# Gated linear attention and two feed-forward layers on one core: right-hand SBUF tiles moved by 32 bytes, and a new set of planned times

## The chip, the cores and the metric

The kernel runs on one core of a Trainium2 chip. The metric is device time in microseconds; lower is better. The kernel before takes 1009.64 us, the median of three runs (1009.35 to 1015.21).

## The reference: what is computed

Three layers, one after the other, on 4 sequences of 768 tokens (3072 tokens in all):

1. Attention with a decaying state, 8 heads of 48: `state = alpha_t * state + k_t v_t^T`, `y_t = q_t state`.
2. A feed-forward layer, 384 to 2048 to 384. Its inner function is a rational one: with `h = x @ w_in`, `g = (a0 + a1 h + a2 h^2 + a3 h^3) / (1 + |b0||h| + |b1| h^2 + 1e-6)`, and the result is `g @ w_out`.
3. A gated feed-forward layer, 384 to 1536 to 384: `silu(x @ w_gate) * (x @ w_val) @ w_out`.

Inputs are random; the weights and `a`, `b` of layer 2 and the weights of layer 3 arrive as 64-bit floats.

## The kernel before, in words

**Work.** Attention is cut into 24 chunks of 128 tokens. For each chunk TensorE turns alpha, k and q around (`tr`, L655), VectorE scans alpha forwards and backwards (L671, L679) and scales k and q (`kt` L687, `qt` L697). TensorE then forms the scores (`scores`, L706), turns `kt` back (`back`, L731) and, in `values`, forms the update of the state (`upd`, L750), scores times v (L755) and state times q (L761). The result goes to DRAM (`xd`).

Layer 2 (`moe1`) takes blocks of 512 tokens. The float32 values are split into a high and a low part, so that each product of float32 matrices is three TensorE products (`mm3`, L840 to L842). One inner tile `f` of a block costs 9 products of 512 columns for `h`, whose streamed (moving) operand is `xt`, some fifteen operations on ScalarE, VectorE and GpSimd, and 9 products of 512 columns for `acc`, whose moving operand is `gg`. The result goes to DRAM (`y1d`).

Layer 3 (`moe2`) takes the same blocks: 72 rounds (6 blocks times 12 inner tiles). A round is 9 products of 512 columns into `pg`, 9 into `pv`, both with `yy` as the moving operand, and 12 products of 384 columns into `po` (L1079 to L1081) with the weights `wo` as the moving operand and `pp` as the stationary one.

**A check beside it.** `bounds` reads alpha and all weights once more: 80 loads named `chk` (L971, 12 of alpha and 68 of weights) into a ring of three buffers. VectorE counts the values in a usable range. For a load of weights these are one extraction (L1013, `chk_e`) and two counts (L984). At the end it sums the counts (L1020, L1021), one small TensorE product adds the partitions (`pf`, L1023), and L1025 writes a `flag`. After the last instruction of the three layers every engine reads the flag (L1197) and branches on it (L1200) past a general program that does not run here.

**Memory.** Pools are opened on the left or the right side of SBUF. On the left lie constants, the 32 weight slots, `xt`, `gg` and the other tiles of `moe1`. On the right lies first `ap` (attention) and, when attention is done, `pb` in its place (`yr`, `yy`, `sg`, `pp` of layer 3). For the first two chunks `kt`, `aa0`, `aa1` and `kn` lie in weight slots on the left (`room`, `early`), later on the right. In the compiled kernel the right side ends at byte 229,344 of a partition, 32 past a multiple of 64; `yr`, `yy`, `sg` and `pp` all start 32 past a multiple of 64, and `xt` and `gg` on one. In `ap` the five tiles of 516 or 517 floats take 2080 bytes each, so that tiles there start partly on multiples of 64, partly 32 past one; `qt` and the later `kt`, `aa` and `kn` start 32 past one.

**Order of the work.** No engine's order is written by hand. Every operation is given to a `Plan` with an engine, a planned duration, what it reads and writes, and a planned time `v`. From these `order` works out a due time for each operation, moved by a bias for its group ("w" weights, "att", "x", "moe"). It then runs a clock of its own: at each step it takes the engine that can start earliest, and on it the operation with the earliest due time among those that are ready by the planned durations. An operation with two possible engines may take the second one only within `THETA` of the lateness of TensorE. The instructions are issued in the order of these planned starts. All engines then work down their queues on the chip, SyncE's DMA queue included, where an issue waits for its tile and holds up those behind it.

One kind of operation also has an absolute floor on that clock, `not_before`: load number k of the check is not planned before `begin + (v - begin) * k / 80`, where

```python
flag = bounds(end_a + 103.59, vs2[-1][0] - 20.0)
```

`vs2[-1][0]` is the planned time of the first round of the last block: `end_a + 5.14 + 60 * P2`, with `P2 = 6.45`. A planned check load lasts 1.1 and is taken to be usable 2.1 later.

The tables `cv` (one planned time for each chunk), `vs` (one for each inner tile of each segment of `moe1`), `MM2`, `EV`, `end_a`, `THETA` and the biases are numbers found by a fit.

Of the kernel before, what the change touches and what calls it, by code (L numbers as in the profile page):

```python
# [9 lines left out]
F32 = mybir.dt.float32  # L10
# [3 lines left out]
ALU = mybir.AluOpType  # L14
# [5 lines left out]
PE, DVE, ACT, POOL, DMA = range(5)  # L20
CAPS = {"w": 99, "early": 9, "att": 3, "h": 5, "acc": 3, "po": 4, "g": 4, "tr": 1, "cv": 1}
HOP = {PE: 0.22, DVE: 0.2, ACT: 0.2, POOL: 0.15, DMA: 2.1}
SAME = {PE: 0.0, DVE: 0.07, ACT: 0.09, POOL: 0.05, DMA: 2.1}
THETA = 48.61


class Buf:
# [7 lines left out]
class Plan:  # L35
# [51 lines left out]
    def order(self):  # L87
# [46 lines left out]
        def ready(e, c):  # L134
            r = c[3]
            if c[2]:
                r = max(r, c[0] + late - THETA)
            if e == DVE and c[4]:
# [216 lines left out]
def gla_moe_moe2_kernel(  # L355
# [15 lines left out]
    nc = tc.nc  # L371
    ctx.enter_context(tc.manual_schedule())
    B, H, S, D = q.shape
# [3 lines left out]
    C = 128  # L377
    C1 = C + 1
    NP = H // 2
    L = NP * C1  # L380
    R = 64 + D
# [13 lines left out]
    plan = Plan()  # L395
    main = ExitStack()
# [4 lines left out]
    ps = main.enter_context(tc.tile_pool(name="ps", bufs=1, space=PSUM))  # L401
    xp = tc.tile_pool(name="xp", bufs=1)
    mp = tc.tile_pool(name="mp", bufs=1)
    ap = tc.tile_pool(name="ap", bufs=1, side="right")
    pb = tc.tile_pool(name="pb", bufs=1, side="right", reuse_waits="tile")
    pb2 = tc.tile_pool(name="pb2", bufs=1, reuse_waits="tile")
# [16 lines left out]
    def new(pool, shape, dt, tag, bufs=1, name=None):  # L423
        b = plan.buf(
            lambda: pool_of(pool).tile(shape, dt, tag=tag, bufs=bufs, name=name or tag), f"{pool}.{tag}", bufs
        )
        if not b.before:
            b.before = after.get(pool, ())
        return b

    def fixed(t):
        b = plan.buf(None)
        b.t = t
        return b
# [26 lines left out]
    A = pools["ap"]  # L461
    NBV = 2
    nat = {}
    for nm in "akqv":
        for i in range(NBV if nm == "v" else 1):
            t = A.tile([128, H, 64], F32, name=f"nat{nm}{i}")
            nc.gpsimd.memset(t[:, :, D:64], 1.0 if nm == "a" else 0.0)
            nat[nm, i] = fixed(t)
    al, seed_f, seed_r = (fixed(A.tile([128, L + 1], F32, name=x)) for x in ("al", "seed_f", "seed_r"))
    for t in (al, seed_f, seed_r):  # L470
        nc.gpsimd.memset(t.t, 0.0)
    nc.gpsimd.memset(seed_f.t[:, 0:L:C1], 1.0)
# [11 lines left out]
    def quad(t):  # L484
        return t.rearrange("p (n c) -> p n c", c=128)
# [148 lines left out]
    def attention(v0, dv, m):  # L634
# [3 lines left out]
        first, last = m % NC == 0, m % NC == NC - 1  # L638
# [11 lines left out]
        def tr(vv, src, name):  # L650
            p4 = bank("tr", name)

            def f():
# [8 lines left out]

        aT = tr(v0, na, "aT")
        plan.op(v0, [(ACT, 0.48, lambda: nc.scalar.copy(per(al.t, 1), quad(aT.t)[0:R]))], (aT,), (al,))
        bb = new("ap", [128, L], F32, "bb")
        bC = new("ap", [128, NP], F32, "bC", 2)
        cc = new("ap", [128, L + 1], F32, "cc")
        kT = tr(v0 + dv, nk, "kT")
        plan.op(
            v0,  # L670
            [(DVE, 1.15, lambda: nc.vector.tensor_tensor_scan(  # L671
                bb.t[0:R], al.t[0:R, 0:L], seed_f.t[0:R, 0:L], 0.0, ALU.mult, ALU.add), True)],
            (al, seed_f), (bb,),
        )
        plan.op(v0, [(DVE, 0.1, lambda: nc.vector.reciprocal(seed_r.t[0:R, C1 : L + 1 : C1], bb.t[0:R, C:L:C1]))],
# [4 lines left out]
                cc.t[0:R, L:0:-1], al.t[0:R, L:0:-1], seed_r.t[0:R, L:0:-1], 0.0, ALU.mult, ALU.add), True)],  # L680
            (al, seed_r), (cc,),
        )
        plan.op(v0, [(ACT, 0.1, lambda: nc.scalar.copy(bC.t[0:R], bb.t[0:R, C:L:C1]))], (bb,), (bC,))
        kt = room("kt")
        plan.op(
            v0 + dv,
# [7 lines left out]
        qt = new("ap", [128, NP, 128], F32, "qt", 2)  # L694
# [6 lines left out]
        sc = [bank("att", f"sc{g}") for g in range(2)]  # L701
# [6 lines left out]
                    start=True, stop=True,  # L708
                )

        plan.op(v0 + 3 * dv, [(PE, 1.1, scores)], (kt, qt), tuple(sc))
        for g in range(2):
            plan.op(
                v0 + 4 * dv,
# [10 lines left out]
        if not last:  # L725
            kn_ps = bank("att", "kn_ps")
            kn = room("kn")

            def back():
                for p in range(NP):  # L730
                    nc.tensor.transpose(quad(kn_ps.t)[:, p, 0:R], kt.t[0:R, p, :], ident[0:R, 0:R])  # L731

            plan.op(v0 + 4 * dv, [(PE, 0.52, back)], (kt,), (kn_ps,))
            plan.op(v0 + 4 * dv, [(ACT, 0.48, lambda: nc.scalar.copy(kn.t[:, :, 0:R], quad(kn_ps.t)[:, :, 0:R]))], (kn_ps,), (kn,))
        yT = bank("att", "yT")
        upd = None if last else bank("att", "upd")
# [4 lines left out]
        def values():  # L741
# [21 lines left out]
                    )  # L763

        plan.op(
            v0 + 5 * dv, [(PE, (0.0 if first else 1.1) + (0.2 if last else 0.7) + 0.9, values)],
            (vn, *aa, qt) + (() if first else (st_s,)) + (() if last else (kn,)), (yT,) + (() if last else (upd,)),
        )
        yo = new("ap", [128, NP, 128], F32, "yo")
# [8 lines left out]
        if last:  # L778
            return
        def bCx():  # L780
            return bC.t[0:R].unsqueeze(2).to_broadcast((R, NP, D))

        if first:
            plan.op(v0 + 6 * dv, [(DVE, 0.27, lambda: nc.vector.tensor_tensor(st_c.t[0:R], u4(), bCx(), ALU.mult))],
# [59 lines left out]
    def moe1(vs, n, part, f0, f1, xt, win, wout):  # L844
# [58 lines left out]
        def second(f, gg):  # L903
# [5 lines left out]

            plan.op(vs[f - f0] + MM2, [(PE, 9 * (T / 2400 + 0.0135), mm2)], (wout[f], gg), tuple(acc))  # L910

# [5 lines left out]
        for z in pend:  # L917
            second(*z)
        vl = vs[-1] + MM2
        for j in range(NJ):  # L920
            ys = new("mp", [128, TMAX], F32, "ys", YS)
            yc = cut_(ys, T)
            if part == 0:
                how = [act(T, lambda j=j, yc=yc: nc.scalar.copy(yc(), acc[j].t[:, 0:T]), 0, False),
                       dve(T, lambda j=j, yc=yc: nc.vector.tensor_copy(yc(), acc[j].t[:, 0:T]))]
                plan.op(vl - EV, how, (acc[j],), (ys,))
            else:
# [104 lines left out]
    def moe2(vs, n, f0, f1, yy, wg, wv, wo):  # L1032
        po = [bank("po", f"po{t}") for t in range(CPB)]

        def first(f):
            v = vs[f - f0]
            pg, pv = bank("g", "pg"), bank("g", "pv")
            for pz, w in ((pg, wg[f]), (pv, wv[f])):

                def gv(pz=pz, w=w):  # L1040
                    for j in range(NJ):
                        s = slice(j * 128, (j + 1) * 128)
                        y = yy[j].t
                        mm3(pz.t, w.t[:, 0, s], w.t[:, 1, s], y[:, 0], y[:, 1], j == 0, j == NJ - 1)

                plan.op(v, [(PE, 2.05, gv)], (w, *yy), (pg, pv) if pz is pg else (pv,))

            cuts = 2 if n == NT // TB - 1 and f == F2 - 1 else 1
            r = []
            for c in range(cuts):  # L1050
                w = TB // cuts
                d = 1 / cuts
                z = slice(c * w, (c + 1) * w)
                sg = new("pb", [128, TB], F32, "sg", 2)
                pp = new("pb", [128, 2, TB], F32R, "pp", 2)
                plan.op(v, [(ACT, 0.08 + 0.42 * d, lambda sg=sg, z=z: nc.scalar.activation(sg.t[:, z], pg.t[:, z], AF.Silu))],  # L1056
                        (pg,), (sg,), last_exp)
                plan.op(v, [(DVE, 0.07 + 0.53 * d, lambda sg=sg, z=z: nc.vector.tensor_tensor(  # L1058
                    sg.t[:, z], sg.t[:, z], pv.t[:, z], ALU.mult))], (sg, pv), (sg,))
                plan.op(v, [(ACT, 0.1 + 0.43 * d, lambda sg=sg, pp=pp, z=z: nc.scalar.copy(pp.t[:, 0, z], sg.t[:, z]))],  # L1060
                        (sg,), (pp,))
                plan.op(
                    v,
                    [(DVE, 0.07 + 0.53 * d, lambda sg=sg, pp=pp, z=z: nc.vector.tensor_tensor(
                        pp.t[:, 1, z], sg.t[:, z], pp.t[:, 0, z].bitcast(F32), ALU.subtract), True)],
                    (sg, pp), (pp,),
                )
                r.append(pp)
            return r

        def second(f, r):
            k = CPB // len(r)
            for c, pp in enumerate(r):

                def mm4(c=c, pp=pp):
                    for t in range(c * k, (c + 1) * k):
                        s = slice(t * 128, (t + 1) * 128)
                        o, w = po[t].t[:, 0:DM], wo[f].t
                        nc.tensor.matmul(o, pp.t[:, 0, s], w[:, 0], start=f == f0, stop=False)  # L1079
                        nc.tensor.matmul(o, pp.t[:, 0, s], w[:, 1], start=False, stop=False)  # L1080
                        nc.tensor.matmul(o, pp.t[:, 1, s], w[:, 0], start=False, stop=f == f1 - 1)  # L1081

                plan.op(vs[f - f0] + 9.60, [(PE, 2.09 / len(r), mm4)], (wo[f], pp), tuple(po[c * k : (c + 1) * k]))

        pend = []
        for f in range(f0, f1):
# [34 lines left out]
            plan.op(vl, [(DMA, 0.6, lambda os=os, r0=r0, q=q: q.dma_start(out[r0 : r0 + 128, :], os.t))], (os,), ())  # L1121


    MM2 = 40.08
    EV = 15.40

    def segments(nf, spec):

# [7 lines left out]

    segs = segments(F1, "0:0-6 1:0-6 2:0-6 3 0:6-16 1:6-16 2:6-16 4 5")

    cv = [-204.83, 163.14, 84.34, -204.08, 123.82, -55.7, -159.63, 143.43, -217.66, -27.45, 250.92, -161.99, -55.72, -358.78, 27.73, -293.03, 7.25, -110.79, -19.49, 75.26, 90.31, 245.52, 120.29, 304.53]
    vs = [  # L1140
# [9 lines left out]
    ]  # L1150
    P2 = 6.45
    end_a = 568.39
    i0 = len(plan.ops)
    plan.bias = {"w": -97.21, "att": 11.01, "x": 131.16, "moe": -55.26}
    plan.group = "att"
    for m in range(NT // C):
        if m == 1:
# [20 lines left out]
    wg, wv, wo = [], [], []  # L1178
# [54 lines left out]
```

## Time and profile before

| | |
|---|---|
| median of 3 runs | 1009.64 us (1009.35 to 1015.21) |
| the profiled execution | 1011.26 us |
| its span, first to last instruction | 1009.5 us |
| mean granted clock of TensorE | 0.993 |
| busy: TensorE, VectorE, ScalarE, GpSimd | 986.1, 773.2, 600.0, 473.3 us |
| chain that ended last | TensorE 86%, ScalarE 5%, VectorE 4%, GpSimd 2% |
| DMA | 113.56 MB, mean 112 GB/s |

The span is the time on the core; the execution's own time is 1.76 us longer. The chain that ended last is followed back from the last instruction, at each step to what released it. A matmul's duration in the profile runs from its start to the modelled end of its last column, while the next one already streams; what a product costs is the distance between starts.

### The profile page before, as it was taken

The numbers are of one execution on the slowest core, as the hardware profiler recorded it, in microseconds if no ns is written. First come the engines' busy times: TensorE is split into PE (matmuls) and PEld (weight loads), VectorE is DVE, ScalarE is ACT, GpSimd is POOL, SyncE is SP. The second block draws the span as 40 slices with busy tenths as digits, with TensorE's granted clock in tenths as the row PEclk, the third lists the DMA queues.
The fourth block names the chain that finished last, engine by engine and source line by source line (L and its number), as shares of the span: only waits on it lengthen the run. The fifth ranks groups of instructions, "written<-read, shape, count | busy, mean of one in ns | idle before, by whom it ended". The sixth has DMA issues, their size and how long they took to land.

```text
span 1009.5 us, 15674 instructions
## 1 busy us (share of the span) xinstructions
PE 986.1 (98%) x5542; PEld 833.5 (83%) x5542; DVE 773.2 (77%) x1455; ACT 600.0 (59%) x1104; POOL 473.3 (47%) x440
## 2 busy tenths in 40 slices
PE   8879899999999999999999999999999999999997
PEld 7768787888888888888888888888888888888886
DVE  6988989999988989789988985349976666666422
ACT  4577899999997869699999763222122113112111
POOL 2268789699977767578999783000000000000000
PEclk9999999999999999999999999999999999999999
DMA  8977754832133241132222651123553544533201
GB/s 174 204 204 181 170 137 117 219 105 63 47 102 87 65 96 55 34 93 58 80 66 94 209 176 38 32 84 123 185 175 124 171 116 133 153 115 109 70 1 34
DMA packets 159462, 113.56 MB, mean 112 GB/s; under 512 B 105232, under 2 KB 132880, under 8 KB 159376
## 3 DMA queue, kind: packets, MB, share of 16 engines
q1 hardware_dynamic: 159088, 112.10, 39.4%
q8 instruction: 45, 0.74, 0.3%
q14 instruction: 41, 0.34, 0.1%
q10 hardware_dynamic: 288, 0.39, 0.1%
HBM read 95.95 MB, written 16.52 MB: 111 GB/s over the span
## 4 chain that ended last, share of the span: by engine, by line
PE 86%; ACT 5%; DVE 4%; POOL 2%; issue 1%; DMA 1%; SPq 0%; ACTq 0%; POOLq 0%; DVEq 0%
PE h L840 6%; PE acc L840 6%; PE acc L842 6%; PE acc L841 6%; PE h L842 6%; PE h L841 6%; PE pv L840 5%; PE po L1081 5%; PE pv L842 5%; PE pv L841 5%; PE pg L842 5%; PE po L1079 5%; PE po L1080 5%; PE pg L841 5%; PE pg L840 5%; PE sc L706 1%
## 5 line engine op out<-in xcount | busy, mean ns | idle before, releaser
L1058 DVE TENSOR_TENSOR sg<-sg,pv 128x512 f32<-128x512 f32 (+1 forms) x73 | 49.5, 680 | 128.6 <-PE pv L842 127.0
L883 POOL TENSOR_TENSOR t<-t,t 128x512 f32<-128x512 f32 x96 | 130.2, 1358 | 34.4 <-ACT t L873 23.6
L1056 ACT ACTIVATE sg<-pg 128x512 f32<-128x512 f32 (+1 forms) x73 | 43.2, 593 | 173.6 <-PE pg L842 172.8
L810 POOL TENSOR_TENSOR gg<-t,gg 128x512 fp32r<-128x512 f32 x96 | 126.7, 1321 | 26.1 <-ACT gg L899 25.1
L1060 ACT CAST pp<-sg 128x512 fp32r<-128x512 f32 (+1 forms) x73 | 45.0, 617 | 134.5 <-DVE sg L1058 124.0
L840 PE MATMUL h<-xt,win 128*128 128x512 f32 x288 | 115.6, 401 | 1.7 <-DVE kt L687 1.6
L840 PE MATMUL acc<-gg,wout 128*128 128x512 f32 x288 | 114.8, 399 | 0.0
L841 PE MATMUL h<-xt,win 128*128 128x512 f32 x288 | 112.8, 392 | 0.7 <-POOL xt L810 0.7
L842 PE MATMUL h<-xt,win 128*128 128x512 f32 x288 | 112.6, 391 | 0.0
L841 PE MATMUL acc<-gg,wout 128*128 128x512 f32 x288 | 112.4, 390 | 0.0
L842 PE MATMUL acc<-gg,wout 128*128 128x512 f32 x288 | 112.3, 390 | 0.0
L1081 PE MATMUL po<-wo,pp 128*128 128x384 f32 x288 | 97.3, 338 | 0.0
L1079 PE MATMUL po<-wo,pp 128*128 128x384 f32 x288 | 97.0, 337 | 0.0
L1080 PE MATMUL po<-wo,pp 128*128 128x384 f32 x288 | 97.0, 337 | 0.0
L840 PE MATMUL pv<-yy,wv 128*128 128x512 f32 x216 | 85.5, 396 | 0.0
L842 PE MATMUL pv<-yy,wv 128*128 128x512 f32 x216 | 85.4, 395 | 0.0
L841 PE MATMUL pv<-yy,wv 128*128 128x512 f32 x216 | 85.2, 395 | 0.0
L842 PE MATMUL pg<-yy,wg 128*128 128x512 f32 x216 | 85.2, 394 | 0.0
L841 PE MATMUL pg<-yy,wg 128*128 128x512 f32 x216 | 85.0, 394 | 0.0
L840 PE MATMUL pg<-yy,wg 128*128 128x512 f32 x216 | 85.0, 393 | 0.0
L889 DVE SCALAR_TENSOR_TENSOR t<-t,h 128x512 f32<-128x512 f32 x96 | 65.3, 681 | 19.5 <-ACT h L888 16.6
L984 DVE TENSOR_SCALAR_CACHE_REDUCE chk_x<-chk_e 128x384 f32<-128x384 uint32 x136 | 75.0, 552 | 3.8
(143 smaller groups left out, 2486.8 us busy)
## 6 DMA issues: line engine op xcount, KB each, us to landing
chk<-in_moe_w_out_dram SPq DMA_DIRECT2D x28, 384.0 KB, 3.4
yr<-y1d SPq DMA_DIRECT2D x36, 256.0 KB, 2.7
xr<-xd SPq DMA_DIRECT2D x27, 256.0 KB, 2.9
y1d<-ys SPq DMA_DIRECT2D x27, 256.0 KB, 2.8
win_st<-in_moe_w_in_dram SPq DMA_DIRECT2D x16, 384.0 KB, 3.8
wout_st<-in_moe_w_out_dram SPq DMA_DIRECT2D x16, 384.0 KB, 3.5
chk<-in_moe_w_in_dram SPq DMA_DIRECT2D x16, 384.0 KB, 3.6
nata<-in_alpha_dram SPq DMA_DIRECT2D x24, 192.0 KB, 3.2
```

The source lines that it names most:

```text
L810: return lambda: eng.tensor_tensor(out_(), in0(), in1().bitcast(F32), ALU.subtract)
L840: nc.tensor.matmul(out_, wh, xh, start=start, stop=False)
L841: nc.tensor.matmul(out_, wh, xl, start=False, stop=False)
L842: nc.tensor.matmul(out_, wl, xh, start=False, stop=stop)
L883: plan.op(v, [pool(T, lambda: nc.gpsimd.tensor_tensor(t1(), t1(), t2(), ALU.mult))], (b1, b2), (b1,))
L889: plan.op(v, [dve(T, lambda: nc.vector.scalar_tensor_tensor(t1(), t1(), ONE_EPS, h(), ALU.add, ALU.mult))], (b1, hb), (b1,))
L984: [(DVE, 0.4, lambda: nc.vector.tensor_scalar(dst(), src(), bound, 0.0, op_, ALU.add, accum_out=cnt.t[:, c : c + 1]))],
L1058: plan.op(v, [(DVE, 0.07 + 0.53 * d, lambda sg=sg, z=z: nc.vector.tensor_tensor(sg.t[:, z], sg.t[:, z], pv.t[:, z], ALU.mult))], (sg, pv), ...
L1060: plan.op(v, [(ACT, 0.1 + 0.43 * d, lambda sg=sg, pp=pp, z=z: nc.scalar.copy(pp.t[:, 0, z], sg.t[:, z]))], (sg,), (pp,))
L1079: nc.tensor.matmul(o, pp.t[:, 0, s], w[:, 0], start=f == f0, stop=False)
L1080: nc.tensor.matmul(o, pp.t[:, 0, s], w[:, 1], start=False, stop=False)
L1081: nc.tensor.matmul(o, pp.t[:, 1, s], w[:, 0], start=False, stop=f == f1 - 1)
```

## The change

It does four things.

- It opens one more pool on the right side, `edge`, before all others, with one tile of 8 floats (32 bytes) that nothing uses. It pads the tiles of 516 and 517 floats to 528 (2112 bytes) and `bC` from 4 floats to 16. By these sizes every tile of the right side starts on a multiple of 64 bytes. The operations on the padded tiles read and write the same elements as before, except that the memsets of `al`, `seed_f` and `seed_r` cover 528 instead of 517.
- It gives the planner other durations for seven kinds of TensorE work: scores 1.1 to 1.31, `back` 0.52 to 0.43, `values` 1.6, 2.7 and 2.2 to 1.71, 2.55 and 2.11 (first, middle, last chunk of a sequence), `pg` 2.05 to 2.08, `pv` 2.05 to 2.04, `po` 2.09 to 2.106.
- It replaces all fitted numbers: `THETA`, `MM2`, `EV`, `cv`, `vs`, `end_a`, the biases.
- Since the check's floors are counted from `end_a`, they move with it.

No operation is added to or taken from the plan, and no dependence between operations is changed.

```diff
-THETA = 48.61
+THETA = 18.97
...
+    edge = main.enter_context(tc.tile_pool(name="edge", bufs=1, side="right"))
+    edge.tile([128, 8], F32, name="edge_fill")
     ap = tc.tile_pool(name="ap", bufs=1, side="right")
...
-    al, seed_f, seed_r = (fixed(A.tile([128, L + 1], F32, name=x)) for x in ("al", "seed_f", "seed_r"))
+    LP = -(-(L + 1) // 16) * 16
+    al, seed_f, seed_r = (fixed(A.tile([128, LP], F32, name=x)) for x in ("al", "seed_f", "seed_r"))
...
-        bb = new("ap", [128, L], F32, "bb")
-        bC = new("ap", [128, NP], F32, "bC", 2)
-        cc = new("ap", [128, L + 1], F32, "cc")
+        bb = new("ap", [128, LP], F32, "bb")
+        bC = new("ap", [128, 16], F32, "bC", 2)
+        cc = new("ap", [128, LP], F32, "cc")
...
-        plan.op(v0 + 3 * dv, [(PE, 1.1, scores)], (kt, qt), tuple(sc))
+        plan.op(v0 + 3 * dv, [(PE, 1.31, scores)], (kt, qt), tuple(sc))
...
-            plan.op(v0 + 4 * dv, [(PE, 0.52, back)], (kt,), (kn_ps,))
+            plan.op(v0 + 4 * dv, [(PE, 0.43, back)], (kt,), (kn_ps,))
...
-            v0 + 5 * dv, [(PE, (0.0 if first else 1.1) + (0.2 if last else 0.7) + 0.9, values)],
+            v0 + 5 * dv, [(PE, 1.71 if first else 2.11 if last else 2.55, values)],
...
-                plan.op(v, [(PE, 2.05, gv)], (w, *yy), (pg, pv) if pz is pg else (pv,))
+                plan.op(v, [(PE, 2.08 if pz is pg else 2.04, gv)], (w, *yy), (pg, pv) if pz is pg else (pv,))
...
-                plan.op(vs[f - f0] + 9.60, [(PE, 2.09 / len(r), mm4)], (wo[f], pp), tuple(po[c * k : (c + 1) * k]))
+                plan.op(vs[f - f0] + 9.60, [(PE, 2.106 / len(r), mm4)], (wo[f], pp), tuple(po[c * k : (c + 1) * k]))
...
-    MM2 = 40.08
-    EV = 15.40
+    MM2 = -144.75
+    EV = -359.58
...
-    cv = [-204.83, 163.14, 84.34, -204.08, ...]
+    cv = [-375.45, 114.26, 18.54, -195.88, ...]
     vs = [
-        [191.6, 209.33, 93.71, 97.69, 62.98, 10.31],
...
+        [-198.53, 208.37, 154.74, -9.96, -38.69, -110.32],
...
-    end_a = 568.39
+    end_a = 636.10
...
-    plan.bias = {"w": -97.21, "att": 11.01, "x": 131.16, "moe": -55.26}
+    plan.bias = {"w": -287.35, "att": -4.77, "x": 198.05, "moe": -59.08}
```

## Rows read from the trace of the kernel before

**Rows 1.** Page, part 1: busy us, share of the span, instructions, by engine.

```profile
PE 986.1 (98%) x5542; PEld 833.5 (83%) x5542; DVE 773.2 (77%) x1455; ACT 600.0 (59%) x1104; POOL 473.3 (47%) x440
```

**Rows 2.** Busy time by stretch: stretch, its us, busy us by engine, clock, DMA.

```profile
0.00:175.00 175.00, 158.34 (x1396) 131.47 (x1397) 153.26 (x245) 130.30 (x266) 117.20 (x129) 0.97 0.70 170
...
545.00:1003.00 458.00, 457.85 (x2184) 397.82 (x2182) 288.71 (x690) 139.48 (x252) 57.71 (x51) 1.00 0.36 114
```

**Rows 3.** TensorE's waits: waiter, releaser, us in total, times, longest.

```profile
PE qT L655 <- ACT yo L770: 3.7, 1, 3.7
PE kT L655 <- ACT aa L715: 2.5, 1, 2.5
```

**Rows 4.** TensorE in order of time, layer 2: start, us, line, operation.

```profile
234.00 0.39 PE L840 MATMUL h<-xt,win 128*128 128x512 f32 x1
...
238.08 0.39 PE L840 MATMUL h<-xt,win 128*128 128x512 f32 x1
```

**Rows 5.** TensorE in order of time, one round of layer 3.

```profile
560.28 0.39 PE L840 MATMUL pg<-yy,wg 128*128 128x512 f32 x1
...
564.47 0.34 PE L1079 MATMUL po<-wo,pp 128*128 128x384 f32 x1
...
566.57 0.39 PE L840 MATMUL pg<-yy,wg 128*128 128x512 f32 x1
```

**Rows 6.** Line 840: durations in ns min/median/max, first and last start in us.

```profile
L840 PE MATMUL h<-xt,win x288: 388/389/775, 58.0 to 540.9; 128*128 128x512 f32 x144
...
L840 PE MATMUL acc<-gg,wout x288: 388/389/504, 81.1 to 555.4; 128*128 128x512 f32 x144
...
L840 PE MATMUL pg<-yy,wg x216: 389/393/497, 543.6 to 993.6; 128*128 128x512 f32 x108
...
L840 PE MATMUL pv<-yy,wv x216: 389/396/399, 549.8 to 997.8; 128*128 128x512 f32 x108
```

**Rows 7.** Chain of waits in order of time, 46 to 112 us: start, us, what.

```profile
46.99 1.10 PE yT L755 x14
...
111.23 1.09 PE yT L755 x16
```

**Rows 8.** The check's tile `chk`: durations in ns, first and last start in us.

```profile
L1013 DVE TENSOR_SCALAR chk_e<-chk x68: 348/354/361, 719.7 to 945.3; 128x384 uint32<-128x384 uint32 x68
L971 SPq DMA_DIRECT2D chk<-in_moe_w_out_dram x28: 327/328/441, 762.2 to 936.6; - x28
...
DMA to landing us min/median/max: 2.9/3.3/5.9
```

**Rows 9.** VectorE in order of time: the check's last load, its sum and flag.

```profile
945.35 0.36 DVE L1013 TENSOR_SCALAR chk_e<-chk 128x384 uint32<-128x384 uint32 x1
...
946.81 0.08 DVE L984 DVE_READ_ACCUMULATOR chk_x<-chk_e 128x1 f32 x1
...
948.79 0.31 DVE L1020 TENSOR_REDUCE tot<-cnt 128x1 f32<-128x160 f32 x1
...
950.33 0.15 DVE L1025 TENSOR_SCALAR flag<-pf 1x1 int32<-1x1 f32 x1
```

**Rows 10.** All engines in order of time: the last product and SyncE's last issue.

```profile
core 0 of [0], span 1009.5 us
...
1002.51 0.34 PE L1081 MATMUL po<-wo,pp 128*128 128x384 f32 x1
...
1002.95 0.34 SPq L1121 DMA_DIRECT2D out_dram<-os  x1
```

**Rows 11.** Lines 1197 and 1200, reading the flag and branching: ns, starts.

```profile
L1197 PEldq TENSOR_LOAD <-flag x1: 491/491/491, 1001.7 to 1001.7; - x1
...
L1200 SPq EVENT_SEMAPHORE  x8: 17/17/17, 1007.6 to 1008.1; - x8
...
L1200 PEldq COMPARE_BRANCH  x1: 4322/4322/4322, 1002.3 to 1002.3; - x1
```

**Rows 12.** VectorE by line, weights split before layer 2: count, busy us, mean ns.

```profile
L560 DVE SCALAR_TENSOR_TENSOR win_x<-win_st,win_e 128x384 uint32<-128x384 uint32 x16 | 8.7, 547 | 0.3
```

More of the change, by code (lines that the diff above doesn't have):

```diff
@@ L671, in attention @@
             [(DVE, 1.15, lambda: nc.vector.tensor_tensor_scan(
-                bb.t[0:R], al.t[0:R, 0:L], seed_f.t[0:R, 0:L], 0.0, ALU.mult, ALU.add), True)],
+                bb.t[0:R, 0:L], al.t[0:R, 0:L], seed_f.t[0:R, 0:L], 0.0, ALU.mult, ALU.add), True)],
             (al, seed_f), (bb,),
@@ L682, in attention @@
         )
-        plan.op(v0, [(ACT, 0.1, lambda: nc.scalar.copy(bC.t[0:R], bb.t[0:R, C:L:C1]))], (bb,), (bC,))
+        plan.op(v0, [(ACT, 0.1, lambda: nc.scalar.copy(bC.t[0:R, 0:NP], bb.t[0:R, C:L:C1]))], (bb,), (bC,))
         kt = room("kt")
@@ L780, in bCx @@
         def bCx():
-            return bC.t[0:R].unsqueeze(2).to_broadcast((R, NP, D))
+            return bC.t[0:R, 0:NP].unsqueeze(2).to_broadcast((R, NP, D))
         if first:
@@ L1137, in gla_moe_moe2_kernel @@
     segs = segments(F1, "0:0-6 1:0-6 2:0-6 3 0:6-16 1:6-16 2:6-16 4 5")
-    cv = [-204.83, 163.14, 84.34, -204.08, 123.82, -55.7, -159.63, 143.43, -217.66, -27.45, 250.92, -161.99, -55.72, -358.78, 27.73, -293.03, 7.25, -110.79, -19.49, 75.26, 90.31, 245.52, 120.29, 304.53]
+    cv = [-375.45, 114.26, 18.54, -195.88, -177.37, -372.3, -233.13, 95.88, -22.27, -5.74, 33.58, -550.05, -62.88, -452.56, -423.12, -64.28, 40.85, -277.16, -205.31, 383.67, 493.41, 454.4, 336.66, 243.74]
     vs = [
[9 rows of a table removed]
[9 rows of a table added]
     ]
     P2 = 6.45
-    end_a = 568.39
+    end_a = 636.10
     i0 = len(plan.ops)
-    plan.bias = {"w": -97.21, "att": 11.01, "x": 131.16, "moe": -55.26}
+    plan.bias = {"w": -287.35, "att": -4.77, "x": 198.05, "moe": -59.08}
     plan.group = "att"
```

16 rows, old and new, of the table vs are left out of this document.

## The prediction, made before the changed kernel was run

> **What bounds the kernel now.** I read the shares first: TensorE is busy 986.1 of 1009.5 us and nothing else comes near it [rows 1, 10]. Then the stretches: in the first 175 us TensorE is busy 158.34, so 16.66 us of idleness lie there; from 545 to 1003 us only 0.15 us are missing [rows 2]. So there are three separate places in which time can change: how long a product takes while TensorE is never idle, the stalls of the first 175 us, and the 6.65 us between the end of the last product at 1002.85 (start 1002.51 plus 0.34) and the end of the span [rows 10]. The early stalls are many small waits; the two longest are 3.7 and 2.5 us [rows 3]. A change on VectorE, ScalarE or GpSimd late in the kernel costs nothing by itself: from 545 us on VectorE is busy 289 of 458 us and ScalarE 139 [rows 2].
>
> **Part one: the addresses.** Layers 2 and 3 use the same kind of product, 128x128 weights and 512 columns, with the moving operand on the left (`xt`, `gg`, on multiples of 64 bytes) or on the right (`yy`, 32 past one). From 234.00 to 238.08 us 18 left-hand products start, 4.08 us, with no gap [rows 4]. The 18 of a round of layer 3 take from 560.28 to 564.47, 4.19 us [rows 5]. The durations say the same: median 389 ns for `h` and `acc`, 393 for `pg`, 396 for `pv` [rows 6]. Their mean excess, 5.5 ns, times 1296 products (72 rounds of 18) is 7.1 us; the starts, 0.11 us times 72 rounds, give 7.9, but that difference carries a rounding of 0.02. I take 7.2. Bounds: nothing, if something other than the address makes `yy` slower, and 7.9. A third value is in the diff: the planned round becomes 2.08 + 2.04 + 2.106 = 6.226, against 6.29 in the trace (560.28 to 566.57) [rows 5]; if these are lengths of the kernel after, 0.064 times 72 rounds is 4.6 us, inside the bounds. That the excess belongs to the address is an inference: it is the one thing in which `yy` differs by construction from `xt` and `gg`.
>
> All of it lies on the path, since TensorE does not idle there. The 12 products into `po` stream from the left and stay.
>
> Here a rule speaks against the change. The Trainium skill (Advanced Engine Details and Errata, section Memory Cachelines) gives SBUF lines of 16 bytes and asks for two accesses to a line for full speed. A tile moved by 32 bytes meets as many such lines as before, so by that rule the gain is nothing, and the sum below would lose its 7.2. The excess in [rows 4 to 6] is against it, though no run here separates address from operand; I carry it as a rival.
>
> In attention the same edit does nothing that I can see. Scores times v stream `aa`, which for the second chunk lies on the left and later on the right: 1.10 us at 46.99, 1.09 at 111.23 [rows 7]. So 0. The far bound is the excess of layer 3, 5.5 ns, on each of some 40 products in 24 chunks, a gain of 5.3 us. VectorE and ScalarE may read the moved tiles faster; they wait in layer 3 anyway. The longer memsets are 2% of three short ones. No slower reading is expected from a rounder address.
>
> **Part two: the check, which nobody meant to move.** The floors of its loads are counted from `end_a`, which goes from 568.39 to 636.10. Before, loads 0 to 79 are planned from 671.98 in steps of 3.357, the last at 937.2, usable by VectorE at 940.4 (1.1 for the load, 2.1 for the hop). In the trace that last extraction starts at 945.35 [rows 9], 57.5 us ahead of the last product's end. At the planned 6.19 a round against 6.29 traced that is 56.6 us on the planner's clock, so its last product ends at about 997. After, the planned rounds add 72 times 0.036, 2.6 us: about 1000, less what the fit saves. But the last two loads now have floors of 1001.5 and 1004.9. They are ordered behind the stores of the output on SyncE's queue, and the stores wait for the last products. Then the flag comes last.
>
> The price, in times of the kernel before. SyncE has issued its last store at 1003.29 (1002.95 plus 0.34) [rows 10]. Two issues of 0.33 follow, each landing 3.3 later: 1006.6 and 1007.0 [rows 8]. VectorE needs 1.54 us a load (945.35 to the end of the count at 946.81 plus 0.08) [rows 9]: 1008.2 and 1009.7. The sum and the flag take from 948.79 to 950.48, of which most is waiting for a busy TensorE; on an idle one I take 1.0: flag at 1010.7. Then TensorE reads it (0.49) and branches (4.32, its next instruction fetched in that time) [rows 11]: 1015.5; and about 1.0 of closing semaphores follow, half of the 1.9 between SyncE's first closing wait at 1007.6 and the end [rows 10, 11]. End 1016.6 instead of 1009.5: **+7.1**. Today the flag is ready at 950.48 and TensorE's load runs at 1001.7, with nothing to wait for. Lower bound 0, if the planner's end moves behind 1009 and the loads stay ahead of the stores; upper bound 8.6, if a third load (floor 998.2) falls behind them too. I take 7.1, since the plan's end would have to move by 9 us for the lower one. On VectorE, what stands behind these counts is only the flag; on SyncE, only each other.
>
> **Part three: the new order.** The planned lengths of a chunk hardly change (middle chunk: 0.21 more, 0.09 and 0.15 less), but the fitted numbers change everything, and the trace cannot show an order that does not exist yet. Bounds: a gain of the 16.66 us that TensorE idles early, which cannot all go, since the first product for layer 2 waits for four chunks of attention until 58.0 us [rows 6]; and a loss of as much, if the fit suits the chip badly. Nearest to zero lies the longest single wait, 3.7 us [rows 3]; I take a gain of 3, by choice.
>
> **The sum.** -7.2 + 7.1 - 3 = -3.1 us. On the profiled execution (span 1009.5 and 1.76 around it, 1011.26) that is 1008.2; the median of the runs lies 1.62 lower, and from it the forecast is **1006.5 us**. One per cent, about what can be told from no change, is 10.1 us: 999.5 and 1019.7 are the borders.
>
> **Rivals.**
> - *The check stays ahead of the end* (the planner's clock runs longer than I infer, or the last loads slip in front of the stores). For it: any fit that looked at the flag would have kept it; against it: the two floors. Time 1009.64 - 7.2 - 3 = 999.4. Chance 0.22, with a spread of 4 us around it, half of it under 999.5.
> - *The address is not the cause*: something else about `yy` slows its products, or the tiles do not come to lie where the sizes say. Against it: 389 against 393 and 396 ns, two operands on one side and one on the other [rows 6]. Time 1009.64 + 7.1 - 3 = 1013.7. Chance 0.08. The Trainium skill's rule on lines of 16 bytes, above, would bring this case.
> - *Slower: the first block of layer 2 comes late.* The place is VectorE before 58 us. In planned time the weights were due 504.6 after the first chunk of attention (191.6 + 97.21 against -204.83 - 11.01); now 459.5 (-198.53 + 287.35 against -375.45 + 4.77). Each weight split ahead of a chunk's scans costs VectorE two operations of 0.55 [rows 12]; eight weights more are 8.8 us, in which TensorE has nothing else to do. Time 1009.64 - 7.2 + 7.1 + 8.8 = 1018.3. It decides against the kernel once the first `h` starts after about 58.1 us, and makes it slower by over 1% past 68. Chance 0.15.
> - *The forecast*: 0.55, own range 1002 to 1011.
>
> **Range and chances.** The range goes from 996 (the lower part of the first rival) to 1015 (the second, and the start of the third), leaving out about 0.05 below and 0.13 above. Faster by over 1%: 0.11 from the first rival and 0.04 from a new order that gains over 10 us: 0.15. Slower by over 1%: a third of the third rival and a little of the second: 0.06. Within 1%: 0.79.
>
> **What would show it.** The address: `pg` and `pv` with a median of 389 ns, 18 products in 4.08 us, and more products in each 25 us of layer 3. The check: extractions of `chk` after the last product, the flag some 8 us behind it, and a span that ends about 14 us after the last product instead of 6.65. The order: TensorE's busy time in the first 175 us, and where the first `h` starts. I am wrong if `pg` stays at 393, if the flag is written before the last product, or if the early idleness changes by more than 8 us.

## The result, and the profile after

The changed kernel takes 1019.75 us (median of 8 runs), the kernel before 1011.07 in the same comparison: a ratio of **1.0083**, 95% interval 1.0068 to 1.0097. It is slower by some 8.4 us. The forecast was 1006.5, with a range up to 1015; the time lies above the range. In kind (within 1%) it was the case given 0.79.

The page after, parts 1 and 4: busy time by engine, and the chain that ended last.

```profile
span 1020.6 us, 15692 instructions
PE 983.9 (96%) x5542; PEld 834.3 (82%) x5542; DVE 768.5 (75%) x1453; ACT 606.8 (59%) x1114; POOL 463.3 (45%) x432
PE 76%; DVE 7%; POOL 7%; ACT 6%; issue 3%; DMA 1%; SPq 0%; POOLq 0%; DVEq 0%; ACTq 0%
```

TensorE does the same 5542 products and is busy 2.2 us less than in [rows 1], yet the span is 11.1 us longer (this profiled execution, 1022.27 us, was the longest of the eight runs). Its idleness is what grew. First one round of layer 3, TensorE in order of time, against [rows 5].

```profile
699.52 0.39 PE L843 MATMUL pg<-yy,wg 128*128 128x512 f32 x1
...
701.60 0.39 PE L843 MATMUL pv<-yy,wv 128*128 128x512 f32 x1
...
703.64 0.33 PE L1082 MATMUL po<-wo,pp 128*128 128x384 f32 x1
...
705.75 0.39 PE L843 MATMUL pg<-yy,wg 128*128 128x512 f32 x1
```

The round has gone from 6.29 to 6.23 us. The 9 products into `pv` now take 2.04, as the aligned products of layer 2 do in [rows 4]; the 9 into `pg` still take 2.08 (2.09 before) and the 12 into `po` 2.11 (2.10 before). The durations say it too, if all three lines are read: `pv` is down to 389, while `pg`, with medians of 393, 394 and 394 ns on L840 to L842 before, now has 389, 395 and 397, no less in the mean.

```profile
L843 PE MATMUL pg<-yy,wg x216: 387/389/467, 553.9 to 998.9; 128*128 128x512 f32 x108
L844 PE MATMUL pg<-yy,wg x216: 389/395/496, 554.1 to 999.1; 128*128 128x512 f32 x108
L845 PE MATMUL pg<-yy,wg x216: 389/397/398, 554.4 to 999.4; 128*128 128x512 f32 x108
...
L843 PE MATMUL pv<-yy,wv x216: 387/389/393, 556.0 to 1003.1; 128*128 128x512 f32 x108
L844 PE MATMUL pv<-yy,wv x216: 389/389/397, 556.2 to 1003.3; 128*128 128x512 f32 x108
```

What keeps 2.08 is not `pg` as such but the place behind `po`. At the head of layer 3, where rounds stand without a `po` between them, `pg` takes 2.04 as well:

```profile
555.96 0.39 PE L843 MATMUL pv<-yy,wv 128*128 128x512 f32 x1
...
558.00 0.39 PE L843 MATMUL pg<-yy,wg 128*128 128x512 f32 x1
...
560.04 0.39 PE L843 MATMUL pv<-yy,wv 128*128 128x512 f32 x1
```

And the four `pv` groups of this trace that follow a `po` (the last at 1001.68) take 2.08.

Then busy time by stretch (TensorE's is the first number after the comma; its idleness is the stretch less that number), as in [rows 2].

```profile
0.00:175.00 175.00, 157.15 (x1400) 130.90 (x1401) 154.56 (x246) 128.20 (x264) 105.56 (x122) 0.98 0.74 179
175.00:600.00 425.00, 419.47 (x2180) 345.10 (x2180) 371.93 (x578) 375.00 (x671) 342.89 (x298) 1.00 0.31 91
```

The first 175 us hold 17.85 us of idleness, 1.2 more than in [rows 2]. Between 175 and 600 us, where the kernel before has next to none, stand 5.53 us. Their waits, in that stretch alone:

```profile
PE pg L844 <- DVE yy L951: 1.9, 2, 1.1
PE h L844 <- POOL xt L813: 1.7, 2, 1.5
PE h L843 <- DVE t L898: 0.8, 2, 0.4
```

At last the end of the span, all engines in order of time, against [rows 9, 10].

```profile
1007.78 0.34 PE L1084 MATMUL po<-wo,pp 128*128 128x384 f32 x1
...
1008.30 0.45 SPq L974 DMA_DIRECT2D chk<-in_moe_w_out_dram  x1
...
1012.22 0.36 DVE L1016 TENSOR_SCALAR chk_e<-chk 128x384 uint32<-128x384 uint32 x1 [2.42 <-DMA chk<-in_moe_w_out_dram]
...
1013.81 0.32 DVE L1023 TENSOR_REDUCE tot<-cnt 128x1 f32<-128x160 f32 x1
...
1014.60 0.15 DVE L1028 TENSOR_SCALAR flag<-pf 1x1 int32<-1x1 f32 x1 [0.28 <-PE pf L1026]
```

The last product ends at 1008.12. SyncE issues the last load of the check 0.18 us later, behind a store of the output; VectorE sits idle 2.42 us for it, and the flag is written 6.5 us after the last product. Then all engines read it and branch (lines 1200 and 1203, as in [rows 11]).

```profile
L1200 PEldq TENSOR_LOAD <-flag x1: 491/491/491, 1014.8 to 1014.8; - x1
...
L1203 PEldq COMPARE_BRANCH  x1: 4082/4082/4082, 1015.4 to 1015.4; - x1
```

From the last product to the end of the span it is 12.5 us, against 6.65.

### The profile page after: what moved, and what is told of

Read it like the earlier page. It is cut to its first block, busy times and chain, and to the rows that moved or that the text cites. A ratio compares the mean times of both kernels' runs of the same rounds, so it can differ in the third digit from the quotient of the medians.

```text
span 1020.6 us, 15692 instructions
## 1 busy us (share of the span) xinstructions
PE 983.9 (96%) x5542; PEld 834.3 (82%) x5542; DVE 768.5 (75%) x1453; ACT 606.8 (59%) x1114; POOL 463.3 (45%) x432
## 4 chain that ended last, share of the span: by engine, by line
PE 76%; DVE 7%; POOL 7%; ACT 6%; issue 3%; DMA 1%; SPq 0%; POOLq 0%; DVEq 0%; ACTq 0%
PE h L843 5%; PE acc L843 5%; PE h L844 5%; PE h L845 5%; PE acc L844 5%; PE acc L845 5%; PE po L1084 4%; PE pg L844 4%; PE pg L845 4%; PE po L1082 4%; PE po L1083 4%; PE pv L845 4%; PE pv L844 4%; PE pv L843 4%; PE pg L843 4%
## 5 line engine op out<-in xcount | busy, mean ns | idle before, releaser
L813 POOL TENSOR_TENSOR gg<-t,gg 128x512 fp32r<-128x512 f32 x96 | 128.9, 1343 | 31.8 <-ACT gg L902 26.0
L887 DVE TENSOR_TENSOR t<-t,h 128x512 f32<-128x512 f32 x96 | 65.3, 681 | 29.9 <-ACT t L883 26.2
L845 PE MATMUL pv<-yy,wv 128*128 128x512 f32 x216 | 84.1, 389 | 0.0
L844 PE MATMUL pv<-yy,wv 128*128 128x512 f32 x216 | 84.1, 389 | 0.0
L843 PE MATMUL pv<-yy,wv 128*128 128x512 f32 x216 | 84.0, 389 | 0.0
```

What stands on the lines that cost most here:

```text
L813: return lambda: eng.tensor_tensor(out_(), in0(), in1().bitcast(F32), ALU.subtract)
L843: nc.tensor.matmul(out_, wh, xh, start=start, stop=False)
L844: nc.tensor.matmul(out_, wh, xl, start=False, stop=False)
L845: nc.tensor.matmul(out_, wl, xh, start=False, stop=stop)
L887: plan.op(v, [dve(T, lambda: nc.vector.tensor_tensor(t4(), t4(), h(), ALU.mult))], (b4, hb), (b4,))
```

## The experiments

Ratios are to the kernel before, run beside each kernel on the same chip. The theory: three independent terms, the addresses (gain), the check behind the end (loss), the new order (loss). The rivals are in the expectations.

### The addresses alone

```diff
 (kernel before)
+    edge = main.enter_context(tc.tile_pool(name="edge", bufs=1, side="right"))
+    edge.tile([128, 8], F32, name="edge_fill")
 ... and the padded tiles of the change
```

> The kernel before with the addresses of the change alone: the 32-byte tile at the right edge and the padded tiles; durations, fitted numbers and floors as before. Theory (address, late check and slower order are three separate terms): layer 3 gets shorter by 72 rounds times 0.058 us, 4.2 us, the rest stays; ratio 0.996, pv at a median of 389 ns, pg partly at 395 as in the changed kernel. Rival one (the moved attention tiles cost the early time): slower by 5 to 8 us, first h after 62 us. Rival two (the address does nothing, the order of the work made pv faster): ratio 1.000, pv at 396.

Measured: **0.9953** (0.9933 to 0.9972), 4.7 us faster. `pv` is at 389, the round at 6.23, the first `h` at 58.07, the time from the last product to the end as before. Rivals one and two fall. TensorE's busy time in its stretches:

```profile
0.00:175.00 175.00, 157.68 (x1392) 0.97 0.70 169
175.00:600.00 425.00, 424.90 (x2227) 1.00 0.33 96
```

### The change with the check's old floors

```diff
 (changed kernel)
-    flag = bounds(end_a + 103.59, vs2[-1][0] - 20.0)
+    flag = bounds(671.98, 940.53)
```

> The changed kernel with the check's floors of the kernel before (671.98 to 940.53) and nothing else changed. Theory: the flag is written before the last product again, and the stretch from the last product to the end of the span shrinks from 12.5 to 6.7 us; 5.8 us less than the changed kernel, so ratio 1.0083 - 0.0057 = 1.0026 to the kernel before. Rival (the tail is long because the changed order ends later on other engines): the stretch stays at 11 to 12.5 us and the ratio at 1.008.

Measured: **1.0011** (0.9995 to 1.0027); 0.0072, or 7.3 us, less than the change. The flag is written at 944.3 us, the last product starts at 1003.80 and the span ends at 1010.5. The theory holds. This kernel and the one before it in this list have the same addresses and the same floors; they differ by lengths and fit alone, and that is 0.0058, or 5.9 us. TensorE's busy time is 981.4 us in both profiles, so that the difference is idleness. Their stretches show where (compare the fence above):

```profile
0.00:175.00 175.00, 158.19 (x1411) 131.53 (x1412) 156.69 (x251) 130.72 (x269) 106.50 (x124) 1.00 0.75 181
175.00:600.00 425.00, 419.09 (x2183) 344.30 (x2182) 371.84 (x577) 375.04 (x671) 342.80 (x299) 1.00 0.31 92
```

Idle to 175 us: 17.32 and 16.81. Idle from 175 to 600: 0.10 and 5.91. The whole loss of the new order lies after 175 us. TensorE's longest waits there:

```profile
PE pg L844 <- DVE yy L951: 2.0, 2, 1.1
PE h L844 <- POOL xt L813: 1.8, 2, 1.6
PE h L843 <- DVE t L898: 1.2, 3, 0.4
```

### The kernel before with the late floors

```diff
 (kernel before)
-    flag = bounds(end_a + 103.59, vs2[-1][0] - 20.0)
+    flag = bounds(739.69, 1008.24)
```

> The kernel before with the check's floors of the changed kernel (739.69 to 1008.24) and nothing else. Theory: the last one or two loads stand behind the stores of the output, the flag comes 6 to 8 us after the last product, the span ends 12 to 14 us after it; 6 to 7 us more than the kernel before, ratio 1.006 to 1.007. Rival (only together with the new order does the check come last): ratio 1.000, flag ahead of the last product.

Measured: 1.0110 (1.0086 to 1.0135), 11 us and more than expected. The rival falls; the size was off, since here three loads are issued after the stores, the extraction of the first waits 2.39 us, and the flag comes 10.2 us after the last product instead of 6 to 8:

```profile
1003.44 1.47 SPq L1121 DMA_DIRECT2D out_dram<-os  x2
1004.95 1.56 SPq L971 DMA_DIRECT2D chk<-in_moe_w_out_dram  x3
```

### The change without the addresses

```diff
 (changed kernel)
-    edge.tile([128, 8], F32, name="edge_fill")
-    LP = -(-(L + 1) // 16) * 16
+    LP = L + 1
 ... and bC back to 4 floats
```

> The changed kernel with the addresses of the kernel before: no edge tile, no padding; durations, fitted numbers and floors of the change. Theory: layer 3 loses its 4.2 us again, pv back at 396 ns; ratio 1.0083 + 0.0042 = 1.0125 to the kernel before, first h still at about 64 us. Rival one (the moved attention tiles cost the early time): faster than the changed kernel by 4 us, ratio 1.004. Rival two (the address does nothing): 1.008, pv at 389.

Measured: 1.0115 (1.0088 to 1.0143), `pv` back at 396. Both rivals fall. The difference to the change, 0.0032, is about as large as its own uncertainty, but lies beside the 0.0047 found with the old order.

### Lengths without the fit, the fit without lengths, THETA back

```diff
 (addresses alone)                     (change, old floors)              (change, old floors)
+ (PE, 1.31, scores) ... all lengths   - (PE, 1.31, scores) ... all      -THETA = 18.97
                                       + (PE, 1.1, scores) ...           +THETA = 48.61
```

> The kernel before with the new addresses and the planner's new lengths; fitted numbers and floors as before. Theory (the 5.8 us of the new order come from the fitted numbers, not from the lengths): as fast as the new addresses alone, ratio 0.995 within 0.002, TensorE idle from 175 to 600 us below 1 us. Rival (the longer scores make the planner place the work differently, whatever the fit): ratio 0.998 to 1.002, idle there 3 us or more.

> The changed kernel with the floors of the kernel before and the planner's old lengths, so the new fitted numbers without the lengths that they were fitted to. Theory (the fitted numbers make the order, the lengths hardly change it): ratio 1.001 within 0.003, the waits for xt and yy still there. Rival (the fit works only with its own lengths): clearly slower than with them, 1.005 or more.

> The changed kernel with the floors of the kernel before and THETA at its old 48.61; the other fitted numbers are the new ones. Theory one (the smaller THETA keeps the splits of xt and yy on their first engine, so TensorE waits for them): the waits of h for xt are gone, TensorE's idleness from 175 to 600 us falls from 5.9 to under 2.5 us, ratio about 0.997. Theory two (the planned times of the tables place the loads and splits late): the idleness stays at 4 us or more, ratio 1.000 to 1.003.

Measured: new lengths with the old fit **1.0145** (1.0112 to 1.0179) instead of 0.995; the new fit with the old lengths **1.0205** (1.0168 to 1.0243) instead of 1.001; the old THETA among the new numbers 1.0091 (1.0056 to 1.0125). My theory failed in the first two, and both theories in the third. TensorE's idleness from 175 to 600 us, which the first theory had below 1 us, is 6.8 with the new lengths alone. The numbers belong together: each set alone costs, and the new fit wins back most of what the new lengths cost.

### Which lengths, and how little is enough

```diff
 (addresses alone)       (addresses alone)            (addresses alone)
+ scores, back, values   + pg 2.08, pv 2.04,          -(PE, 0.52, back)
  at their new lengths     po 2.106                   +(PE, 0.50, back)
```

> The kernel before with the new addresses and the new planned lengths of attention's products alone (scores, back, values); layer 3's lengths, fit and floors as before. Theory one (the longer scores are what upsets the old fit, by a planned 0.21 us in 24 chunks): ratio about 1.014, as with all lengths. Theory two (layer 3's lengths do it): ratio 0.995.

> The kernel before with the new addresses and the new planned lengths of layer 3's products alone (pg, pv, po); attention's lengths, fit and floors as before. Theory one (attention's lengths upset the old fit): ratio 0.995, TensorE idle under 1 us from 175 to 600 us. Theory two (layer 3's do): ratio about 1.014.

> The kernel before with the new addresses and one planned length moved by 0.02 us (back 0.52 to 0.50); all else as before. Theory one (the planner's order is sensitive, and the old fit holds for its own inputs alone, so that any other input costs): ratio 1.003 or more, against 0.9953 without the nudge. Theory two (only a length that is wrong for the chip, as scores at 1.31 against 1.09 traced, costs): ratio 0.995 within 0.002.

Measured: attention's lengths 1.0169 (1.0140 to 1.0197), as theory one has it; layer 3's 0.9987 (0.9955 to 1.0019), between the theories and nearer to the first. The nudge of 0.02 us on one planned length: **1.0312** (1.0281 to 1.0342), the slowest kernel of all. TensorE's stretches with the nudge:

```profile
0.00:175.00 175.00, 157.63 (x1342) 0.96 0.72 172
175.00:600.00 425.00, 404.23 (x2108) 0.98 0.27 75
```

TensorE's idleness in the first 175 us is as before (17.4 us); from 175 to 600 us it is 20.8 us instead of 0.1. That is not the whole loss: this profile's span is 36.9 us longer than that of the addresses alone (1042.4 against 1005.5), and 14.9 of them are longer busy time, 996.3 us for the same 5542 products against 981.4, at a mean granted clock of 0.984 against 0.993. A length need not be wrong for the chip to cost. Three of these four changes of the planner's lengths (all of them, attention's alone, the nudge) cost clearly with the old fit; that layer 3's alone cost, 0.0034 above the addresses alone, is not shown, since the noise of the two comparisons is as large.

### Is it the operand's address?

```diff
 (kernel before)
+    pools["xp"].tile([128, 8], F32, name="left_fill")
```

> The kernel before with a 32-byte tile in front of the tiles of layer 2 on the left, so that xt and gg start 32 past a multiple of 64 bytes; the order of the work is the same. Theory (a moving operand off a multiple of 64 makes a product of 512 columns slower): h and acc go from a median of 389 ns to 393 to 396, 18 products from 4.08 to about 4.19 us, and 96 pairs of 9 and 9 cost 96 times 0.10, some 10 us more: ratio 1.009 to 1.011. Rival (something else about yy, or about the right side): h and acc stay at 389, ratio 1.000.

Measured: **1.0093** (1.0058 to 1.0128). Same order, same sides, only the tiles of layer 2 (`xt`, `gg` and the working tiles beside them) lie 32 bytes further on, and `h` and `acc` become as slow as `pg` and `pv` were in [rows 6]:

```profile
L842 PE MATMUL h<-xt,win x288: 389/396/775, 57.6 to 551.0; 128*128 128x512 f32 x144
...
L842 PE MATMUL acc<-gg,wout x288: 392/396/505, 82.0 to 565.7; 128*128 128x512 f32 x144
```

That settles that the place of the tiles counts: 32 bytes further on, the same products take longer. Whose address counts in layer 3 was asked of two more kernels (one run each, so that their whole times, 1015.1 and 1011.0 us, say little):

```diff
 (addresses alone)
-pp = new("pb", [128, 2, TB], F32R, "pp", 2)
+pp: a tile of 2 * TB + 16 floats, used from float 8 on     (the other kernel: the same for yy)
```

> The kernel before with the new addresses, but pp, the stationary operand of the products into po, put 32 past a multiple of 64 bytes; yy stays on a multiple. What is open: with the new addresses alone the 12 products into po take 2.106 us against 2.101 before, and the 9 into pg 2.081 where pv takes 2.040. Theory (the address of the stationary operand sets these lengths): po and pg move by 10 ns or more in a round. Rival (only the moving operand's address counts): po 2.106, pg 2.081, pv 2.040 as before.

> The kernel before with the new addresses, but yy, the moving operand of pg and pv, put 32 past a multiple of 64 bytes; pp stays on a multiple. The mirror image of the kernel with pp off. Theory one (the moving operand's own address slows its products, as with xt and gg): pv goes from 2.040 to about 2.10 for nine. Theory two (in layer 3 only pp's address counts, and it slows the whole round): pv stays at 2.040, pg at 2.081, po at 2.106.

One round with `pp` off:

```profile
702.03 0.39 PE L843 MATMUL pg<-yy,wg 128*128 128x512 f32 x1
...
704.12 0.39 PE L843 MATMUL pv<-yy,wv 128*128 128x512 f32 x1
...
706.21 0.34 PE L1083 MATMUL po<-wo,pp 128*128 128x384 f32 x1
...
708.32 0.40 PE L843 MATMUL pg<-yy,wg 128*128 128x512 f32 x1
```

And one with `yy` off:

```profile
698.60 0.39 PE L843 MATMUL pg<-yy,wg 128*128 128x512 f32 x1
...
700.68 0.40 PE L843 MATMUL pv<-yy,wv 128*128 128x512 f32 x1
...
702.79 0.33 PE L1083 MATMUL po<-wo,pp 128*128 128x384 f32 x1
...
704.89 0.39 PE L843 MATMUL pg<-yy,wg 128*128 128x512 f32 x1
```

Both rounds take 6.29 us, as long as the round before in [rows 5]. For `yy`, theory one holds: beside `yy` only `yr` moved, which TensorE does not read.

The kernel with `pp` off does not show what it was built for. Its two `pp` buffers are 64 bytes longer each, so `yy`, which lies below them in the same pool, starts 128 bytes lower than with the addresses alone; it is still on a multiple of 64. And its very first nine products into `pg` already take 2.09 us:

```profile
546.71 0.40 PE L843 MATMUL pg<-yy,wg 128*128 128x512 f32 x1
...
548.80 0.39 PE L843 MATMUL acc<-gg,wout 128*128 128x512 f32 x1
```

With the addresses alone they take 2.04 (544.26 to 546.30). No `pp` had been written by then; the first write of one starts at 555.9:

```profile
L1064 ACT CAST pp<-sg x73: 407/621/656, 555.9 to 1005.0; 128x512 fp32r<-128x512 f32 x71, 128x256 fp32r<-128x256 f32 x2
```

So `pp` cannot be what slows these products, and the new place of `yy` is what is left. Whether the address of `pp` counts at all is not shown. Nor is "a multiple of 64" the rule: in the compiled kernels `xt`, `gg` and, with the addresses alone, `yy` start 448 bytes past a multiple of 512 and are fast, `yy` at 320 past one is slow (the kernel with `pp` off), and so is everything at 480 (`yy` in the kernel before, `xt` and `gg` when moved); with `yy` off its five buffers start at 160 to 416. Which places are fast in general, and whether it is the place itself or the distance to another tile, stays open.

## Why the prediction was wrong, point by point

**The sum in a line.** Forecast: addresses -7.2, check +7.1, order -3. Measured between kernels that differ by one of them, on 1011 us: addresses -4.7 (0.9953), order +5.9 (0.9953 to 1.0011), check +7.3 (1.0011 to 1.0083); together +8.5. By the intervals each of the three is good to some 2 to 3 us. Two steps failed: the sign of the order's term, which was off by 8.9 us, and the size of the addresses' term, which was off by 2.5.

**The check: right, its number partly by luck.** The floors counted from `end_a` put the last load behind the stores; old floors alone take 0.0072 off. In the profile the end moved by 5.8 us (12.5 against 6.65), since one load fell behind the stores where I had counted two; TensorE's branch took 4.08 us, against 4.32 in [rows 11]. By runs it was 7.3, so that the 7.1 lies closer than its own working, with two loads, deserved. The lever was in the diff: a number that looked like a fitted priority was also the origin of an absolute time.

**The addresses: right in kind, too large.** The step that failed is the inference that the excess is the moving operand's alone and so falls away entirely. It fell away for `pv`, 2.10 to 2.04, and for a `pg` that does not follow `po`. In nearly every round `pg` does follow `po`, and there it kept 2.08, while `po` kept 2.11; so a round won 0.06 us instead of 0.11. The lengths that the diff gives the planner, 2.08 + 2.04 + 2.106, are those of the round after to the hundredth; I had their 4.6 us as a third value and passed over it. Why the products behind `po` keep an excess stays open. Against the Trainium skill's lines of 16 bytes (Advanced Engine Details and Errata, Memory Cachelines) the measurement decides: with that line a move by 32 bytes should change nothing, and it changes `h` from 389 to 396 ns.

**The new order: wrong in sign, and this decided.** The 3 of "I take a gain of 3, by choice" was put near the longest single wait [rows 3], but no row gave it a sign. I had drawn both bounds from the idleness of the first 175 us, and none from the rest, with 0.1 us of idleness up to 545 us and 0.15 after it. It was the other way round: the first 175 us did not change (17.3 and 16.8 us idle, same addresses), and the stretch without stalls lost 5.8. A tuned stretch at no idleness cannot gain from a new order, only lose; the bounds should have been drawn from that. The third rival had its sign and nearly its sum (1018.3), but not its place: in the changed kernel the first `h` did start 6 us later, at 63.92, and by 175 us that was made up to 1.2 us. Why the new numbers make `xt`, `t` and `yy` late is not shown.

**Attention's addresses: right, nothing to see.** With the addresses alone the early idleness (17.3 us against 16.7) and the first `h` (58.1 against 58.0) stay as good as they were.

**The version that beats both** is the addresses with nothing else: 0.9953.

## What to carry to other kernels

A planner's fitted numbers are good for one set of inputs: here a planned length changed by 0.02 us without a new fit cost 3%. So bring a gain in addresses or sizes in without touching the planner's inputs, and time a new fit against the old one with that gain in both. And before a fitted number is moved, look for everything that is counted from it.

## What was not expected of the hardware

- Moving the streamed operand by 128 bytes can cost as much as by 32: with `yy` 128 bytes lower, and still on a multiple of 64, the first nine `pg` products took 2.09 us instead of 2.04; with `xt` and `gg` 32 bytes further on, nine products of layer 2 took 2.10.
- An excess passes on to the group behind. With the new addresses the nine products behind `po` took 2.08 us, whichever they were, and 2.04 elsewhere. In the kernel before, the nine `acc` products behind a slow `pg` took 2.07 (554.03 to 556.10), and with the new addresses 2.04, though their own tiles had not moved.
- From the flag (1014.60) to the end of the span (1020.6) it is 6 us, of which TensorE's branch takes 4.08. The kernel before has a branch as long, 4.32 [rows 11], but it starts at 1002.3, beside the last products and stores, and waits for no flag.
